# Six token blocks taken as three pairs, with seven half-width products for eight in their first channel product

## The chip, the core and the metric

The kernel runs on one core of a Trainium2 chip. Its time is the device time of that core in microseconds (us), the median of several runs. TensorE (PE) multiplies and adds up into PSUM banks; VectorE (DVE) and ScalarE (ACT) read PSUM and the core's on-chip memory SBUF, and GpSimd (POOL) here works on SBUF only; SyncE (SP) issues the transfers (DMAs), in order, from one queue. The engines run side by side and wait for each other on semaphores.

## The reference

`S` is 576, `B` is 8, `DM` is 512. Attention in chunks of 64 positions gives x; a token mixer and a channel mixer follow:

```python
scores = scale * np.matmul(q_c, k_c.transpose(0, 1, 2, 4, 3))
attn = np.exp(scores - np.max(scores, axis=-1, keepdims=True))
attn = attn / (np.sum(attn, axis=-1, keepdims=True) + 1e-09)
x = np.matmul(attn, v_c)                              # then [8, 576, 512]
h = np.maximum(x.transpose(0, 2, 1) @ w_tok1, 0.0) @ w_tok2   # 576 -> 256 -> 576
u = x + h.transpose(0, 2, 1)
out = u + np.maximum(u @ w_ch1, 0.0) @ w_ch2          # 512 -> 1536 -> 512
```

All data is 32-bit float. In the large products each operand is split into a high part and the rest (`xh`, `xl` and so on), and three of the four partial products are added up in PSUM (the tuple `THREE`), so each 128x128 by 128xN product costs three matmul instructions.

## The kernel before

**Stages.** Batch 0 goes first, in two halves of 288 positions, while the weights arrive and are converted and split. The positions of the other seven batches are one row of 4032, cut into `BLOCKS`: seven of 512 columns and one of 448. For each block, `turn` makes u by the second token product (`block_tok2`, line 562, ACT copy 573, rest on DVE or POOL 574). Then twelve steps `f`, one for each 128 of the 1536 hidden channels, run: `ch1` (line 584) multiplies four 128-channel tiles of u with the step's weights, 4 x 3 = 12 matmuls into one `ps_c1` bank; ACT takes the relu out of the bank (`gh`, line 595) and DVE the rest (`gl`, line 596); `ch2` (line 626), again 12 matmuls, adds the step into four `ps_acc` banks, one for each 128 output channels. `ch2` of a step runs one step behind `ch1`. At the end DVE adds u's high part to each bank (line 634), POOL its rest (line 636), and SP writes the result (line 637); for the last block POOL has added both parts of u beforehand (line 620), so only line 634 is left.

**Attention.** A tile of 128 rows needs a burst (`attention`): TensorE's 32 small matmuls for the scores of tile k (line 325) and 32 for the values of tile k-1 (line 337), both in the one `ps_at` bank pair. DVE then does the maximum, the subtraction, the scaled x of the older tile, two transposes, a sum and two small operations (lines 298 to 315, 348, 416), ACT the exponential (305); the transposed tiles go to DRAM and come back (`far`, `pf`, `xt`). Five or four bursts stand in each of the first six blocks (`SLOTS`). The first token product `tok1` (line 491) of a batch runs when its tiles are there.

**What sets the order.** TensorE's and SP's instructions stand in the order in which the program writes them. From batch 0's end on, DVE, ACT and POOL are ordered by a planner that places each instruction by its own estimate of when it can start; they then run in that fixed order, each waiting at its head. `ps_c1` has two banks, `ps_acc` four.

## Time and profile before

| | us |
|---|---|
| median of 3 runs (793.21 to 795.62) | 794.05 |
| the profiled execution, its time | 792.71 |
| its span, first to last instruction | 790.6 |
| TensorE busy | 774.0 |
| VectorE / ScalarE / GpSimd busy | 349.3 / 237.9 / 108.2 |

A span is what the trace sees of an execution. In views by group, `out<-in xcount | busy, mean ns of one | idle before`; "PE" is matmuls, "PEld" the loading of their weights, which runs beside them. Matmuls overlap: a "mean" of one is longer than the distance from one start to the next.

### The profile page before, as it was taken

To read this page: it belongs to the slowest core of one execution; us is meant where nothing else is said; L and a number is where in the kernel's file an instruction comes from. 1 tells how busy PE (TensorE), PEld (TensorE's weight loads), DVE (VectorE), ACT (ScalarE), POOL (GpSimd) and SP (SyncE) were. 2 spreads that over 40 slices of the span, in tenths; PEclk is the share of its full clock that TensorE was granted. 3 is DMA by queue.
4 is the path that set the end of the run, shared out by engine and by line. 5 is a ranking of instruction groups with operands and counts; after the bars stand their busy time and mean duration, and the time that the engine had idled before them with its cause. 6 is when DMAs were issued, how large, how long until landed. Compare 5 with 4: busy or idle time off the path is not lost.

```text
span 790.6 us, 14145 instructions
## 1 busy us (share of the span) xinstructions
PE 774.0 (98%) x5857; PEld 652.1 (82%) x5857; DVE 349.3 (44%) x627; ACT 237.9 (30%) x418; POOL 108.2 (14%) x94
## 2 busy tenths in 40 slices
PE   6899999999999999999999999999999999999998
PEld 4489898888888888888888888888888888888997
DVE  5888846654435341544444434535353314114112
ACT  6899834322221221222322222222212211101110
POOL 0000002310013010401040103100030103003300
PEclk8999999999999999999999999999999999999999
DMA  9934434343413440344413430535134201000101
GB/s 351 407 131 173 131 125 124 93 152 128 153 47 114 141 162 19 108 149 137 135 59 120 150 108 27 174 124 161 44 114 134 80 1 54 0 1 15 40 0 47
DMA packets 66415, 87.60 MB, mean 111 GB/s; under 512 B 7792, under 2 KB 41328, under 8 KB 66352
## 3 DMA queue, kind: packets, MB, share of 16 engines
q1 hardware_dynamic: 66352, 86.71, 33.0%
q8 instruction: 46, 0.75, 0.4%
q14 instruction: 17, 0.14, 0.1%
HBM read 59.81 MB, written 25.95 MB: 108 GB/s over the span
## 4 chain that ended last, share of the span: by engine, by line
PE 86%; DMA 5%; ACT 4%; DVE 3%; SPq 1%; issue 1%; DVEq 0%; ACTq 0%
PE acc L626 34%; PE ps_c L584 33%; PE ps_t L562 6%; PE ps_t L491 5%; DMA raw_c<-in_wc 2%; PE ps_sv L325 2%; PE ps_sv L337 2%; PE ps_t L534 1%; DMA v<-in_vo 1%; DMA far<-blocks 1%; ACT low L165 1%; PE ps_t L528 1%; SPq L359 1%; ACT low L174 1%; ACT wtop L164 1%
## 5 line engine op out<-in xcount | busy, mean ns | idle before, releaser
L626 PE MATMUL acc<-gh,kept_c 128*128 128x512 f32 (+2 forms) x960 | 272.8, 372 | 1.7 <-ACT gh L595 1.0
L584 PE MATMUL ps_c<-uh,kept_c 128*128 128x512 f32 (+1 forms) x768 | 234.1, 386 | 0.0
L596 DVE SCALAR_TENSOR_TENSOR gl<-ps_c,gh 128x512 fp32r<-128x512 f32 (+2 forms) x108 | 71.0, 657 | 315.4 <-ACT gh L595 315.4
L626 PEld LDWEIGHTS acc<-gh,kept_c 128*128 128x128 f32 x960 | 170.5, 188 | 30.9 <-ACT gh L595 1.5
L626 PE MATMUL acc<-gl,kept_c 128*128 128x512 f32 (+2 forms) x480 | 170.7, 369 | 0.0
L584 PEld LDWEIGHTS ps_c<-uh,kept_c 128*128 128x128 f32 x768 | 144.1, 188 | 27.5
L584 PE MATMUL ps_c<-ul,kept_c 128*128 128x512 f32 (+1 forms) x384 | 148.3, 386 | 0.0
L595 ACT ACTIVATE gh<-ps_c 128x512 fp32r<-128x512 f32 (+2 forms) x108 | 61.6, 570 | 283.6 <-PE ps_c L584 283.6
L626 PEld LDWEIGHTS acc<-gl,kept_c 128*128 128x128 f32 x480 | 88.0, 188 | 14.3
L434 POOL TENSOR_TENSOR xl<-x,xh 128x512 fp32r<-128x512 f32 x28 | 36.8, 1314 | 358.4 <-ACT xh L433 303.8
L584 PEld LDWEIGHTS ps_c<-ul,kept_c 128*128 128x128 f32 x384 | 72.1, 188 | 14.3 <-DVE ul L574 0.4
L574 POOL TENSOR_TENSOR ul<-u,uh 128x512 fp32r<-128x512 f32 (+1 forms) x16 | 20.9, 1307 | 256.3 <-ACT uh L573 219.3
L562 PE MATMUL ps_t<-kept_t,rh 128*128 128x448 f32 (+7 forms) x224 | 48.6, 311 | 0.0
L376 ACT COPY pt<-pf 128x512 f32<-128x512 f32 x31 | 19.2, 620 | 91.1 <-DMA pf<-far 91.1
L584 PE MATMUL ps_c<-both,kept_c 128*128 128x288 f32 x288 | 44.8, 302 | 0.2
L305 ACT ACTIVATE pr<-pr 128x512 f32<-128x512 f32 x36 | 22.7, 630 | 61.0 <-DVE pr L301 61.0
L584 PEld LDWEIGHTS ps_c<-both,kept_c 128*128 128x128 f32 x288 | 39.7, 188 | 1.5 <-ACT g L592 0.4
L562 PEld LDWEIGHTS ps_t<-kept_t,rh 128*128 128x128 f32 x224 | 37.6, 190 | 1.5
L636 POOL TENSOR_TENSOR o<-o,ul 128x512 f32<-128x512 f32 x28 | 38.5, 1404 | 1.2 <-DVE o L634 1.1
L568 DVE TENSOR_TENSOR u<-ps_t,xt 128x512 f32<-128x512 f32 (+1 forms) x32 | 21.8, 682 | 34.9 <-PE ps_t L562 34.7
L573 ACT CAST uh<-u 128x512 fp32r<-128x512 f32 (+1 forms) x32 | 19.5, 614 | 52.8 <-DVE u L568 52.8
L562 PE MATMUL ps_t<-kept_t,rl 128*128 128x448 f32 (+7 forms) x112 | 34.8, 311 | 0.0
(87 smaller groups left out, 701.3 us busy)
## 6 DMA issues: line engine op xcount, KB each, us to landing
qk<-in_qk SPq DMA_DIRECT2D x36, 512.0 KB, 3.9
far<-blocks SPq DMA_DIRECT2D x63, 256.0 KB, 2.1
raw_c<-in_wc SPq DMA_DIRECT2D x24, 512.0 KB, 9.3
pf<-far SPq DMA_DIRECT2D x124, 64.0 KB, 2.0
out<-o SPq DMA_DIRECT2D x28, 256.0 KB, 2.0
v<-in_v SPq DMA_DIRECT2D x27, 256.0 KB, 4.1
xt<-far SPq DMA_DIRECT2D x100, 64.0 KB, 2.0
v<-in_vo SPq DMA_DIRECT2D x9, 260.0 KB, 8.0
```

The lines of the kernel that those rows point to most:

```text
L305: nc.scalar.activation(out=pr, in_=pr, func=AF.Exp, scale=1.0 / float(D) ** 0.5)
L434: nc.gpsimd.tensor_tensor(out=xl, in0=t["x"], in1=xh.bitcast(F32), op=ALU.subtract)
L491: nc.tensor.matmul(ps, lhsT=lhsT, rhs=rhs, start=(n == 0 and q == 0), stop=(n == len(mt) - 1 and q == len(terms) - 1),)
L562: nc.tensor.matmul(ps[:, at:at + n], lhsT=lhsT[:, cols], rhs=rhs, start=(q == 0), stop=(q == len(terms) - 1),)
L568: nc.vector.tensor_tensor(out=u.rearrange("p (i c) -> p i c", c=BK), in0=ps[:, :width].rearrange("p (i c) -> p i c", c=BK), in1=block_x(k) ...
L573: nc.scalar.copy(out=uh[m], in_=u)
L574: (nc.vector if m in UL_ON_VECTOR else nc.gpsimd).tensor_tensor(out=ul[m], in0=u, in1=uh[m].bitcast(F32), op=ALU.subtract)
L584: nc.tensor.matmul(ps[:, :width], lhsT=weights["c1", f][:, wi, k * P:(k + 1) * P], rhs=u[ui][k], start=(k == 0 and q == 0), stop=(k == NDT ...
L595: nc.scalar.activation(out=gh, in_=ps[:, :width], func=AF.Relu)
L596: nc.vector.scalar_tensor_tensor(out=gl, in0=ps[:, :width], scalar=0.0, in1=gh.bitcast(F32), op0=ALU.max, op1=ALU.subtract)
L626: nc.tensor.matmul(accs[e], lhsT=weights["c2", f][:, wi, e * P:(e + 1) * P], rhs=g[gi], start=(f == 0 and q == 0), stop=(f == NFC - 1 and ...
L636: nc.gpsimd.tensor_tensor(out=o, in0=o, in1=u[1][e].bitcast(F32), op=ALU.add)
```

## The change

The first two blocks keep the old scheme. The six others are taken two at a time, in columns 512, 512 and 480 wide. For a pair of blocks and a pair of steps (2p, 2p+1), the first channel product is a 2x2 by 2x2 block product: two token blocks by two halves of 256 channels, times two halves by two steps. It is done by seven half-size products (`product`, 6 matmuls each into one `ps_c1` bank), with four combinations of u's quarters (`mix_pair`) and four of the weights' quarters (`add_sums`, `split_sums`). POOL and ACT make the weights' combinations during the two first blocks; SP writes all seven operands of each of the six step pairs to DRAM (`dump`, 42 tiles of 256 KB), and reads one before each product into a ring of 8 (`load_product`, 126 reads). The seven products are put together outside PSUM: `snap` copies two of them to SBUF on ACT, `plus` adds five more from PSUM on DVE and two sums in SBUF on POOL. The pair's first block gets its hidden steps at once (`c11`, `c21`), with its `ch2` in halves of 6 matmuls between the products; the second block's twelve are kept in SBUF (`later`) and its `ch2` follows in `pair_end`. The token weights are written to DRAM and read again for the pairs. Bursts stand nearer together, at places `step(0)` to `step(7)` of each p (14 in the two first blocks, 9 and 4 in the first two pairs' products), values two tiles behind scores (`LAG`).

```diff
 N = 512
-BLOCKS = [(k * N, min(N, (B - 1) * S - k * N)) for k in range(-(-(B - 1) * S // N))]
-SLOTS = {0: (1, 3, 5, 7, 9), 1: (2, 4, 6, 8), 2: (1, 3, 5, 7, 9)}
+SINGLE = 2
+PAIRS = 3
+BLOCKS = [(k * N, N) for k in range(2 * PAIRS)]
+LAST = ((B - 1) * S - 2 * PAIRS * N) // 2
+BLOCKS += [(2 * PAIRS * N + k * LAST, LAST) for k in range(2)]
+KH = 2 * P
+RING = 8
+LAG = 2
+BURSTS = (2, 5, 9, 13, 17, 21, 24, 27, 30, 32, 35, 38, 40, 43)
+PAIR_BURSTS = {0: (2, 7, 12, 17, 22, 27, 32, 37, 42), 1: (4, 12, 20, 28), 2: ()}
+PAIR_GAPS = (1, 3)
+SUMS = ((2, 5, 7), (8, 11, 13), (14, 17, 19), (24, 27, 29), (30, 33, 35), (36, 39, 41))
...
+    def before(k):
+        if LAG <= k:
+            with in_turn():
+                attn_t(order[k - LAG])
     def attention(k):
         i = order[k] if k < len(order) else None
-        j = order[k - 1] if k else None
-        if j is not None:
-            attn_t(j)
+        j = order[k - LAG] if k >= LAG else None
         attn_both(i, j)
+        if k + 2 < len(order):
+            attn_load(order[k + 2])
+        load_waiting(3)
         if i is not None:
             attn_p(i)
-            attn_far(i)
+            tiles[i]["far"] = far_out(tiles[i]["pr"])
             attn_z(i)
         if j is not None:
             attn_o(j)
             attn_end(j)
...
+    def behind(k):
+        if k < len(order):
+            t = tiles[order[k]]
+            t["pf"] = pool.tile([P, 4, NHP, BK], F32, tag="pf", name="pf", bufs=2)
+            far_in(t.pop("far"), t["pf"])
+        if LAG <= k:
+            j = order[k - LAG]
+            with in_turn():
+                stack_end(j)
+                if j in SOON:
+                    attn_split(j)
+    calls = {"before": before, "burst": attention, "behind": behind}
+    def plan_bursts(bursts, first, lead, trail):
+        at = {}
+        for k, s in enumerate(bursts, first):
+            for kind, t in (("before", s - lead), ("burst", s), ("behind", s + trail)):
+                at.setdefault(t, []).append((kind, k))
+        return at
...
+    def add_sums(p):
+        fa, fb = weights["c1", 2 * p], weights["c1", 2 * p + 1]
...
+        s = pool.tile([P, 4, KH], F32, tag="sums", name="sums", bufs=1)
+        for out_, in0, in1, op in (
+            (1, b[:, 0], b[:, 1], ALU.add), (0, s[:, 1], a[:, 0], ALU.subtract),
+            (2, a[:, 0], b[:, 0], ALU.subtract), (3, a[:, 1], s[:, 0], ALU.subtract),
+        ):
+            nc.gpsimd.tensor_tensor(out=s[:, out_], in0=in0, in1=in1, op=op)
...
+    def split_sums(p):
+        fa, fb, s = sources[p]
+        parts = pool.tile([P, 4, 2, KH], F32R, tag="sparts", name="sparts", bufs=1)
+        nc.scalar.copy(out=parts[:, :, 0], in_=s)
+        nc.gpsimd.tensor_tensor(
+            out=parts[:, :, 1], in0=s, in1=parts[:, :, 0].bitcast(F32), op=ALU.subtract
+        )
...
+    def dump(n):
+        for key, src in dumps[:n]:
+            stored[key] = wide.tile([P, 2, KH], F32, tag="w{}_{}".format(*key), name="w")
+            nc.sync.dma_start(out=stored[key], in_=src.bitcast(F32))
...
+    def load_product(upto):
+        for i in range(len(ring), min(upto, len(products))):
+            w = pool.tile([P, 2, KH], F32, tag="ring", name="ring", bufs=RING)
+            nc.sync.dma_start(out=w, in_=stored[products[i]])
+            ring.append(w)
...
+    def product(i, u, width):
+        load_product(i + RING - 1)
+        ps = ps_c1.tile([P, 512], F32, tag="c1", name="ps_p")[:, :width]
+        w = ring[i]
+        for j in range(2):
+            for q, (wi, ui) in enumerate(THREE):
+                nc.tensor.matmul(
+                    ps, lhsT=w[:, wi, j * P:(j + 1) * P].bitcast(F32R), rhs=u[ui][j],
+                    start=j == 0 and q == 0, stop=j == 1 and q == 2,
+                )
+        return ps
...
+    def mix_pair(k, rs, m):
...
+        for h, l in ((0, 0), (1, 0), (0, 1), (1, 1)):
...
+            us[h, l] = block_mix(k + l, rs, 2 * h + m, ps)
...
+        def combine(a, b):
+            t = pool.tile([P, N], F32, tag="ts", name="ts", bufs=4)[:, :width]
+            nc.vector.tensor_tensor(out=t, in0=a, in1=b, op=ALU.subtract)
+            return t
...
+            nc.scalar.copy(out=hi, in_=u)
+            engine.tensor_tensor(out=lo, in0=u, in1=hi.bitcast(F32), op=ALU.subtract)
...
+        split(0, us[0, 0], nc.vector)
+        split(1, us[1, 0], nc.gpsimd)
+        t1 = combine(us[0, 1], us[0, 0])
+        split(3, t1, nc.gpsimd)
+        t2 = combine(us[1, 1], t1)
+        split(2, t2, nc.gpsimd)
+        split(4, combine(us[1, 1], us[0, 1]), nc.gpsimd)
+        split(5, combine(us[1, 0], t2), nc.gpsimd)
+        split(6, us[1, 1], nc.gpsimd)
+        own["base"][m] = us[0, 1]
...
+    def finish(e, acc, at, width, base, rest=None):
+        o = pool.tile([P, N], F32, tag="o", name="o", bufs=8)[:, :width]
+        nc.vector.tensor_tensor(out=o, in0=acc, in1=base, op=ALU.add)
+        if rest is not None:
+            nc.gpsimd.tensor_tensor(out=o, in0=o, in1=rest, op=ALU.add)
+        nc.sync.dma_start(out=out[e, :, at:at + width], in_=o)
...
+    def snap(ps, width):
+        s = pool.tile([P, N], F32, tag="snap", name="snap", bufs=2)[:, :width]
+        nc.scalar.copy(out=s, in_=ps)
+        return s
...
+    def plus(a, b, width, tag, engine=None):
+        c = pool.tile([P, N], F32, tag=tag, name=tag, bufs={"g2": NFC, "sum": 3}.get(tag, 1))[:, :width]
+        (engine or nc.vector).tensor_tensor(out=c, in0=a, in1=b, op=ALU.add)
+        return c
...
+    def split_sum(c, width, relu=True):
+        gh, gl = g_parts(width)
+        nc.scalar.activation(out=gh, in_=c, func=AF.Relu)
+        nc.vector.scalar_tensor_tensor(
+            out=gl, in0=c, scalar=0.0, in1=gh.bitcast(F32), op0=ALU.max, op1=ALU.subtract
+        )
+        return gh, gl
...
+    def pair(n, rs):
...
+        for p in range(NFC // 2):
+            i = (n * (NFC // 2) + p) * 7
...
+            low, high = range(2), range(2, NDT)
+            p1 = snap(product(i, own[0], width), width)
+            c11 = plus(product(i + 1, own[1], width), p1, width, "c11")
+            step(0)
+            if pend is not None:
+                ch2_half(2 * p - 1, pend, accs, low, False, False)
+            step(1)
+            u2 = plus(product(i + 2, own[2], width), p1, width, "sum")
+            g1 = split_sum(c11, width)
+            p5 = snap(product(i + 3, own[3], width), width)
+            step(2)
+            if pend is not None:
+                ch2_half(2 * p - 1, pend, accs, high, False, False)
+            step(3)
+            u3 = plus(product(i + 4, own[4], width), u2, width, "sum")
+            u4 = plus(p5, u2, width, "sum", nc.gpsimd)
+            later[2 * p + 1] = plus(p5, u3, width, "g2", nc.gpsimd)
+            c21 = plus(product(i + 5, own[5], width), u3, width, "c21")
+            step(4)
+            ch2_half(2 * p, g1, accs, low, p == 0, False)
+            step(5)
+            pend = split_sum(c21, width)
+            later[2 * p] = plus(product(i + 6, own[6], width), u4, width, "g2")
+            step(6)
+            ch2_half(2 * p, g1, accs, high, p == 0, False)
+            step(7)
+            if p == NFC // 2 - 1 and n + 1 < PAIRS:
+                load_tokens(("t1", "half"))
+        ch2_half(NFC - 1, pend, accs, range(NDT), False, True)
+        for e in range(NDT):
+            h, m = divmod(e, 2)
+            finish(e, accs[e], S + at, width, own[h][0][m].bitcast(F32), own[h][1][m].bitcast(F32))
...
+    def pair_end(n, rs, later):
...
+        for f in range(NFC):
...
+            g, ahead = ahead, split_sum(later[f + 1], width) if f + 1 < NFC else None
+            ch2_half(f, g, accs, range(NDT), f == 0, f == NFC - 1)
+            for b, at_f in zip(mixes, (3, 5)):
+                if f == at_f:
+                    rs[b] = [tok1(b, m) for m in range(NT1)]
...
+            load_waiting(2)
+            if n + 1 < PAIRS and f in (6, 8):
+                load_waiting(99)
+                mix_pair(k + 2, rs, (f - 6) // 2)
+        for e in range(NDT):
+            h, m = divmod(e, 2)
+            if h == 0:
+                finish(e, accs[e], S + at, width, own["base"][m])
+            else:
+                finish(e, accs[e], S + at, width, own[6][0][m].bitcast(F32), own[6][1][m].bitcast(F32))
...
+    for k in range(SINGLE):
+        at, width = BLOCKS[k]
         accs, pend = [], None
         for f in range(NFC):
-            g = ch1(u, f, width=width)
-            if f in steps:
-                attention(done)
...
-            if pend is not None:
-                ch2(*pend)
-            pend = (S + at, width, u, f, g, accs)
-            if end and k + 1 < len(BLOCKS):
...
+            for half in range(2):
+                if half == 0:
+                    g = ch1(u, f, width=width)
+                elif pend is not None:
+                    ch2(*pend)
+                if half == 1:
+                    pend = (S + at, width, u, f, g, accs)
...
+                now = 2 * (NFC * k + f) + half
+                for kind, at_k in single_events.get(now, ()):
+                    calls[kind](at_k)
+                dump(2 if now > 36 else 1)
+                for p, (add, cut, put) in enumerate(SUMS):
+                    if now in (add, cut):
+                        with in_turn():
+                            (add_sums if now == add else split_sums)(p)
+                    if now == put:
+                        dump_sums(p)
+        dump(len(dumps))
+        if k == 0:
+            u = turn(1, rs)
+        else:
+            mix_pair(SINGLE, rs, 1)
+        ch2(*pend)
+    for n in range(PAIRS):
+        later = pair(n, rs)
+        pair_end(n, rs, later)
```

The three places on which the numbers rest, as the instructions are ordered. Names ending in a number are single buffers. **First, TensorE around a burst**, before, in step 2 of a block: the end of `ch1` (`ps_c1`), the burst (`ps_sv`), the start of `ch2` (`acc`).

```order
L584 MATMUL ps_c1_6394<-uh_6237,kept_c1_2_647 128x512 x2
L584 MATMUL ps_c1_6394<-ul_6241,kept_c1_2_647 128x512
L584 MATMUL ps_c1_6394<-uh_6238,kept_c1_2_647 128x512 x2
L584 MATMUL ps_c1_6394<-ul_6242,kept_c1_2_647 128x512
L325 MATMUL ps_sv_6413<-qk_6083 64x64 x16
L337 MATMUL ps_sv_6413<-v_5956,pt_6411 64x64 x16
L626 MATMUL acc_6378<-gh_6374,kept_c2_1_686 128x512 x2
L626 MATMUL acc_6378<-gl_6375,kept_c2_1_686 128x512
L626 MATMUL acc_6379<-gh_6374,kept_c2_1_686 128x512 x2
L626 MATMUL acc_6379<-gl_6375,kept_c2_1_686 128x512
```

And after, in the first pair, p = 1, at the burst behind the sixth product: the end of that product (`ps_p_4912`), the burst, half a `ch2`, and the seventh product (`ps_p_4989`).

```order
L996 MATMUL ps_p_4912<-bh_4568,ring_4753 128x512 x2
L996 MATMUL ps_p_4912<-bl_4569,ring_4753 128x512
L342 MATMUL ps_sv_4921<-qk_4689 64x64 x16
L354 MATMUL ps_sv_4921<-v_4104,pt_4893 64x64 x16
L1071 MATMUL acc_4604<-gh_4867,kept_c2_2_820 128x512 x2
L1071 MATMUL acc_4604<-gl_4868,kept_c2_2_820 128x512
L1071 MATMUL acc_4605<-gh_4867,kept_c2_2_820 128x512 x2
L1071 MATMUL acc_4605<-gl_4868,kept_c2_2_820 128x512
L996 MATMUL ps_p_4989<-bh_4464,ring_4828 128x512 x2
L996 MATMUL ps_p_4989<-bl_4465,ring_4828 128x512
L996 MATMUL ps_p_4989<-bh_4572,ring_4828 128x512 x2
L996 MATMUL ps_p_4989<-bl_4573,ring_4828 128x512
```

Twelve matmuls into one bank have become six, and a burst stands between short pieces.

**Second, DVE around a burst**, before: the twelve-matmul bank's rest (`gl`) stands ahead of and behind the burst's eight operations.

```order
L596 SCALAR_TENSOR_TENSOR gl<-ps_c_4773,gh 128x512
L298 TENSOR_REDUCE mx<-ps_sv 128x8
L301 TENSOR_TENSOR pr<-ps_sv,mx 128x2x4x64
L416 TENSOR_TENSOR x<-ps_sv,zs 128x512
L348 STREAM_TRANSPOSE blocks<-pr 128x4x4x32
L311 TENSOR_REDUCE zs<-pr 128x8
L348 STREAM_TRANSPOSE blocks<-x 128x4x4x32
L314 TENSOR_SCALAR zs<-zs 128x8
L315 RECIPROCAL zs<-zs 128x8
L596 SCALAR_TENSOR_TENSOR gl<-ps_c_4873,gh 128x512
```

And after, around the burst shown above. `sum` is the fifth product's addition, `c_4919` the sixth's, `g_4996` the seventh's.

```order
L1094 TENSOR_TENSOR sum<-ps_p,sum 128x512
L1094 TENSOR_TENSOR c_4919<-ps_p,sum 128x512
L1100 SCALAR_TENSOR_TENSOR gl<-c_4919,gh 128x512
L315 TENSOR_REDUCE mx<-ps_sv 128x8
L318 TENSOR_TENSOR pr<-ps_sv,mx 128x2x4x64
L433 TENSOR_TENSOR x<-ps_sv,zs 128x512
L365 STREAM_TRANSPOSE blocks<-pr 128x4x4x32
L328 TENSOR_REDUCE zs<-pr 128x8
L365 STREAM_TRANSPOSE blocks<-x 128x4x4x32
L1094 TENSOR_TENSOR g_4996<-ps_p,sum 128x512
L331 TENSOR_SCALAR zs<-zs 128x8
L332 RECIPROCAL zs<-zs 128x8
```

Three additions that read product banks have come in, one of them behind the burst's larger operations, and `gl` now reads SBUF (`c_4919`) where it read a bank.

**Third, the end**, before, on DVE (the last `gl`s, then the four output additions) and on POOL:

```order
L596 SCALAR_TENSOR_TENSOR gl<-ps_c_7712,gh 128x448
L596 SCALAR_TENSOR_TENSOR gl<-ps_c_7741,gh 128x448
L596 SCALAR_TENSOR_TENSOR gl<-ps_c_7770,gh 128x448
L596 SCALAR_TENSOR_TENSOR gl<-ps_c_7799,gh 128x448
L634 TENSOR_TENSOR o<-acc,o 128x448 x4
```

```order
L636 TENSOR_TENSOR o<-o,ul 128x512 x4
L574 TENSOR_TENSOR ul<-u,uh 128x448 x2
L636 TENSOR_TENSOR o<-o,ul 128x512 x2
L620 TENSOR_TENSOR o<-uh,ul 128x448 x4
L636 TENSOR_TENSOR o<-o,ul 128x512 x2
```

And after, DVE and POOL (its last six are four of the pair's first block and two of the second):

```order
L1100 SCALAR_TENSOR_TENSOR gl<-g_8312,gh 128x480
L1100 SCALAR_TENSOR_TENSOR gl<-g_8445,gh 128x480
L1100 SCALAR_TENSOR_TENSOR gl<-g_8417,gh 128x480
L1082 TENSOR_TENSOR o<-acc,u 128x480 x2
L1082 TENSOR_TENSOR o<-acc,bh 128x480 x2
```

```order
L1094 TENSOR_TENSOR sum<-snap,sum 128x480
L1094 TENSOR_TENSOR g_8312<-snap,sum 128x480
L1094 TENSOR_TENSOR sum<-snap,sum 128x480
L1094 TENSOR_TENSOR g_8417<-snap,sum 128x480
L1084 TENSOR_TENSOR o<-o,bl 128x480 x6
```

Two of the last four outputs now end with an addition on POOL, which before was done ahead of them.

More of the change, by code (lines that the diff above doesn't have):

```diff
@@ L468, in batch_tiles, with open_x, load_waiting, close_tile @@
+    def open_x(*blocks):
+        for k in blocks:
+            opened.add(k)
+            waiting.extend((i, k) for i in ended)
+    waiting = []
+    def load_waiting(n):
+        while waiting and n > 0:
+            n -= load_x(*waiting.pop(0))
+    ended = []
+    def close_tile(i):
+        ended.append(i)
+        waiting.extend((i, k) for k in sorted(opened))
     def batch_tiles(b):
@@ new lines, in load_tokens @@
+    def load_tokens(kinds):
+        for key, d in tokens.items():
+            if (key if key == "half" else key[0]) not in kinds:
+                continue
+            w = pool.tile(list(d.shape), F32, tag="again_" + "_".join(map(str, key)), name="again", bufs=1)
+            nc.sync.dma_start(out=w, in_=d)
+            w = w[:, :, :].bitcast(F32R)
+            if key == "half":
+                half_low[:] = [w[:, c] for c in range(2)]
+            elif key[0] == "t1":
+                for j in range(key[2]):
+                    weights["t1", key[1] + j] = w[:, :, j * DT:(j + 1) * DT]
+            else:
+                weights[key] = w
@@ new lines, in ch2_half, with new_accs @@
+    def ch2_half(f, g, accs, es, start, stop):
+        for e in es:
+            for q, (wi, gi) in enumerate(THREE):
+                nc.tensor.matmul(
+                    accs[e], lhsT=weights["c2", f][:, wi, e * P:(e + 1) * P], rhs=g[gi],
+                    start=start and q == 0, stop=stop and q == 2,
+                )
+    def new_accs(width):
+        return [ps_acc.tile([P, 512], F32, tag="acc", name="acc")[:, :width] for _ in range(NDT)]
+    def finish(e, acc, at, width, base, rest=None):
[4 more added lines that the diff above has]
+        nc.sync.dma_start(out=out[e, :, at:at + width], in_=o)
```

250 lines of the change are left out of this document (184 added, 66 removed).

## The prediction

> **What bounds the kernel now.** I read the busy table first, then busy time by stretch (columns: stretch, length, busy PE, PEld, DVE, ACT and POOL with counts, granted clock, DMA share, GB/s).
>
> ```profile
> span 790.6 us, 14145 instructions
> PE 774.0 (98%) x5857; PEld 652.1 (82%) x5857; DVE 349.3 (44%) x627; ACT 237.9 (30%) x418; POOL 108.2 (14%) x94
> ```
>
> ```profile
> 0.00:20.00 20.00, 14.01 (x225) 9.39 (x225) 10.29 (x25) 12.27 (x20) 0.91 (x10) 0.83 0.92 351
> 20.00:40.00 20.00, 16.42 (x194) 9.72 (x183) 15.96 (x36) 16.16 (x30) 0.00 (x0) 1.00 1.03 407
> 0.00:139.00 139.00, 126.51 (x1300) 107.50 (x1300) 100.10 (x209) 97.98 (x185) 9.85 (x18) 0.98 0.58 207
> 139.00:787.00 648.00, 647.50 (x4562) 544.63 (x4558) 248.51 (x418) 139.96 (x233) 98.31 (x77) 1.00 0.28 90
> 231.00:318.00 87.00, 87.00 (x640) 72.91 (x640) 34.41 (x58) 19.07 (x32) 14.52 (x11) 1.00 0.31 99
> ```
>
> All of TensorE's idle time but 0.5 us lies in the first 139 us and the last 4. Between, TensorE is the path, so a matmul less is time less, as long as nothing new makes it wait. Other engines have room there: in the block from 231 to 318 DVE is busy 34 of 87 us, POOL 15. The pace of TensorE stands in the chain of waits (start, length, what):
>
> ```profile
> 575.00 5.44 PE ps_c L584 x24
> ...
> 585.88 0.62 PE ps_sv L325 x32
> 586.51 0.47 PE ps_sv L337 x32
> ...
> 728.60 4.86 PE ps_c L584 x24
> ...
> 787.08 0.62 DVE o L634
> ```
>
> A matmul of 512 columns takes 5.44/24 = 0.2267 us, one of 448 takes 4.86/24 = 0.2025; on the line between them 480 columns take 0.2146. A burst takes 1.09.
>
> **Term 1, the matmuls removed: -24.0 us.** Before, the two channel products are 7 x 12 x 24 = 2016 matmuls of 512 and 288 of 448: 457.0 + 58.3 = 515.3 us. After, the two single blocks have 576 of 512; each of two pairs has 6 x 7 x 6 = 252 in products and 288 in `ch2`, so 1656 of 512 in all; the third pair has 540 of 480: 375.4 + 115.9 = 491.3. The other work of TensorE is kept: 27 bursts, 14 `tok1`, the second token product in equally many pieces. The first 139 us lose nothing on TensorE, so their idle time stays.
>
> **Term 2, the end: +2.1 us.** Before, the last DVE addition (787.08) is followed by its transfer. Now the third and fourth of the last outputs each get one more addition on POOL: 1.40 us for 512 columns (the POOL row on line 636 below), so 1.32 for 480. The third's can start when its DVE addition ends, 0.6 before the last one's, and the two follow each other: 2 x 1.32 - 0.6 = 2.1 later than now.
>
> **Term 3, waits for a product's bank: +2.4 us.** Groups (line, operation, count | busy, mean ns), then single instructions of DVE and ACT (start, length):
>
> ```profile
> L595 ACT ACTIVATE gh<-ps_c 128x512 fp32r<-128x512 f32 x84 | 50.2, 598 | 232.3 <-PE ps_c L584 232.3
> ...
> L634 DVE TENSOR_TENSOR o<-acc,uh 128x512 f32<-128x512 f32 x28 | 18.5, 684 | 0.4
> ...
> L434 POOL TENSOR_TENSOR xl<-x,xh 128x512 fp32r<-128x512 f32 x28 | 36.8, 1314 | 358.4 <-ACT xh L433 303.8 <-issue 32.8 <-PE acc L626 21.9
> ...
> L636 POOL TENSOR_TENSOR o<-o,ul 128x512 f32<-128x512 f32 x28 | 38.5, 1404 | 1.2 <-DVE o L634 1.1
> ```
>
> ```profile
> 241.66 0.39 PE L584 MATMUL ps_c<-ul,kept_c 128*128 128x512 f32 x1
> ...
> 242.15 0.60 ACT L595 ACTIVATE gh<-ps_c 128x512 fp32r<-128x512 f32 x1 [4.13 <-PE ps_c L584]
> ...
> 546.07 0.68 DVE L298 TENSOR_REDUCE mx<-ps_sv 128x8 f32<-128x512 f32 x1
> ...
> 550.23 0.20 DVE L315 RECIPROCAL zs<-zs 128x8 f32<-128x8 f32 x1
> ...
> 572.99 1.38 DVE L634 TENSOR_TENSOR o<-acc,uh 128x512 f32<-128x512 f32 x2
> 574.29 1.50 DVE L574 TENSOR_TENSOR ul<-u,uh 128x512 fp32r<-128x512 f32 x1
> 575.71 1.28 DVE L634 TENSOR_TENSOR o<-acc,uh 128x512 f32<-128x512 f32 x2
> ```
>
> A bank is handed over 0.10 us after its last matmul (242.05 to 242.15). It was emptied by `gh` and `gl` while 24 other matmuls, 5.4 us, ran; now a product's bank is wanted again after one product and half a `ch2`, 12 x 0.2267 = 2.72 us. Without a burst that fits: hand-over 0.10, then `snap` 0.60 (a copy out of PSUM, taken as `gh`) or a DVE addition with one PSUM operand, 0.69, then 0.10 back. At a pair's start, where there is no `ch2` yet, 1.36 against 0.9 still fits, and DVE has added the outputs of the block before by the first product's end.
>
> With a burst it is nearer. DVE is held 550.43 - 546.07 = 4.4 us. Take the burst of the rows in the change. With T the end of its matmuls, the sixth product ended at T - 1.09; `c` ends at T - 0.3, `gh` at T + 0.3, `gl` at T + 1.05; `mx`, `pr`, `x`, two transposes and `zs` take 4.0 more (the 4.4 without its two small last operations), so `g` ends at T + 5.75 and its bank is free at T + 5.85. TensorE asks for it after four pieces of 1.36, at T + 5.44: it waits 0.4 us. A burst after a step pair's second product gives the same for `sum`. There are six bursts at these two places (two in the first pair, the four of the second); at the other seven the next addition stands right behind `x`, or its bank has been emptied ahead of the burst. 6 x 0.4 = 2.4. Low end 0. High end: the addition behind `gl` and a whole burst at all 13 places, 3.1 us each as worked out in the rivals, 41 us. The written order is near the low end.
>
> `gl` now has both operands in SBUF. The 1.50 us row is such an operation beside POOL's work, and the additions from PSUM beside it stay at 0.69. If POOL were adding during the six `gl`s, they would cost 0.8 each, +4.9; but POOL's two sums of a step pair end about 0.6 us before that `gl` starts (the second follows the fifth product by 0.8 + 1.4), so I take 0.69. The Trainium skill (SBUF — State Buffer, "SBUF: two separate sides") says that a VectorE operation with two SBUF inputs and a GpSimd one exclude each other for a whole instruction. By it such a `gl` could take 0.69 + 1.40, and the six would give +8.4; the row shows 1.50, less than that.
>
> **Costed at nothing, with the cover.** *Weights' sums*: for each step pair POOL does two additions of 512, four of 256 and one of 1024 columns, about 3 x 2.6 = 8 us in proportion to the columns of the `xl` row, 48 for six, in two blocks, of which the second had POOL busy 14.5 of 87 us; without that room the first token products would wait for `xl`. *u's combinations*: in the second half of a mix POOL does six rests, and beside the first pair four output additions, 6 x 1.31 + 4 x 1.40 = 13.5 us, wanted for the seventh product about 16 us after they can start (the end of the mix, `ch2`, six products, half a `ch2` and a burst); each us beyond that is one us of waiting, at three pairs. *ACT* gains 36 snaps, 18 casts and six wide ones, about 40 us of 650. *DVE* gains 90 additions, 62 us: in the first pair, 99.6 us long, it has 5 additions and 2 `gl` in each of six step pairs and 9 bursts, 42 x 0.69 + 9 x 4.4 = 69 us (99.6 is 6 x 66 x 0.2267 + 9 x 1.09). *SP* gains 186 DMAs of 0.43 us:
>
> ```profile
> 239.41 4.54 SPq L637 DMA_DIRECT2D out<-o  x4
> ...
> 245.95 0.43 SPq L257 DMA_DIRECT2D qk<-in_qk  x1
> ```
>
> ```profile
> v<-in_v SPq DMA_DIRECT2D x27, 256.0 KB, 4.1
> ...
> raw_c<-in_wc SPq DMA_DIRECT2D x24, 512.0 KB, 9.3
> ```
>
> That is 80 us of issuing in some 630. The new transfers are 168 of 256 KB and 8 MB of token weights, 52 MB; with the 58 MB that 90 GB/s make in 648 us it is some 175 GB/s, and the start ran at 207. A ring read is issued seven products before its use, 12 to 15 us; a 256 KB read lands in 4.1. The attention tile's return (`pf`) moves behind loads and a second `far` on SP, but is used two bursts later, not one.
>
> **The sum.** 792.7 - 24.0 + 2.1 + 2.4 = 773.2 for the profiled execution; the median of the runs is 1.3 above it, so 794.05 - 19.5 = 774.5.
>
> **Rivals.** *The banks decide (slower).* The addition that reads a product stands behind `gl` and a burst on DVE: `gl` ends at T + 1.05, the burst's large operations 4.0 later, the addition 0.69, the way back 0.1, so the bank is free at T + 5.85. At most places it is wanted two pieces behind the burst, at T + 2.72: 3.1 us for each of 13 bursts, 41 us, and 794.05 - 24.0 + 2.1 + 41 = 813. It makes the change slower from 21.9/13 = 1.7 us a burst. For it: 4.4 us of burst against 2.72. Against: the additions are spread among the burst's operations.
> *The ring is late.* SP waits in order; outputs held it 4.54 us, and a read as slow as `raw_c` takes 9.3. Together 13.8, at a pair's start against 12.2, and some waits for DVE on top: 3 to 4 us at three pair starts, 785. Against: 4.1 is the size's own row.
> *The clock.* 20 to 40 us has 3.6 us of idle time at clock 1.00, 0 to 20 has 6.0 at 0.83. If the first pair's 99.6 us of short pieces ran at 0.83, that is 99.6 x (1/0.83 - 1) = 20.4 us: 795, no change. The Trainium skill (TensorE: Matmul & The Clock Gate, "A second HAM failure mode: psum-queue depth-cycling") tells of a matmul kernel whose clock swung because it idled briefly at each change of PSUM bank. Waits of 0.4 us are far from either row.
> *The matmuls saved are not time saved*: reading weights from the ring would have to cost 19.5/756 = 26 ns a matmul; 794. Against: PEld, busy 544.6 of 648 us, already runs beside the matmuls, and the ring's weights have the same shape.
>
> **How the numbers follow.** Forecast 0.74 (its own range 769.5 to 780), ring late 0.11, banks 0.09, clock 0.03, nothing saved 0.03. A change within 0.3%, about 2.4 us, is no change to this measurement. Faster: 0.74 + 0.11 = 0.85; same 0.06; slower 0.09. The low end of the range is term 1 alone, 770.0, less 0.5 for the scatter of the runs; the high end takes in the late ring, 785.
>
> **What would show it.** PE busy should fall to about 750, with 756 matmuls on the product line 0.2267 us apart. In the pairs, idle time of PE under about 5 us, ended by DVE's additions, and near the step-4 and step-0 bursts; more than 22 us makes me wrong. PE's waits for the ring's DMAs: none. Granted clock 1.00 there. The chain of waits should end with POOL's addition, about 2 us more behind the last matmul. If idle time lies in the two single blocks, the sums or the writing on SP are to blame.

## The result: half a per cent slower, not 2.5% faster

Measured over 16 executions each, the change takes 798.48 us (median, 791.52 to 803.76) and the kernel before 793.27 (791.57 to 796.23): 1.0054 times the time, 95% interval 1.0034 to 1.0074. The ratio is of means and leaves out the change's two longest executions (803.59 and 803.76 us), which count as slow, so it lies a little below that of the medians. Forecast were 774.5 us. The profiled execution of the change took 795.3 us, its span is 793.5.

The head of the page of the change:

```profile
span 793.5 us, 14680 instructions
PE 760.0 (96%) x5749; PEld 636.0 (80%) x5749; DVE 445.3 (56%) x735; ACT 269.9 (34%) x478; POOL 234.3 (30%) x190
PE 74%; DMA 7%; DVE 7%; SPq 4%; ACT 3%; POOL 3%; issue 2%; POOLq 0%; DVEq 0%; ACTq 0%
```

The 108 matmuls are gone (5857 to 5749), but TensorE's busy time fell by 14.0 us, not 24, and its idle time rose from 16.6 to 33.5. In the chain of waits (third line) TensorE's part, 86% before, is 74%; DMA, DVE and SP's queue have gained. Busy time by stretch (columns as before: stretch, length, busy PE, PEld, DVE, ACT, POOL, granted clock, DMA share, GB/s), first the kernel before:

```profile
152.00:231.00 79.00, 78.53 (x643) 63.93 (x642) 34.46 (x64) 19.88 (x33) 10.26 (x9) 1.00 0.41 127
231.00:340.00 109.00, 109.00 (x800) 91.35 (x800) 46.26 (x77) 24.36 (x40) 22.68 (x17) 1.00 0.32 103
```

and the change:

```profile
152.00:231.00 79.00, 76.00 (x674) 61.24 (x673) 38.59 (x68) 22.61 (x37) 32.55 (x30) 0.96 0.72 236
231.00:340.00 109.00, 103.47 (x946) 85.48 (x945) 56.56 (x95) 31.20 (x53) 41.42 (x35) 1.00 0.67 214
340.00:380.00 40.00, 33.18 (x276) 27.88 (x276) 28.02 (x37) 12.38 (x21) 27.21 (x18) 0.91 0.38 125
380.00:787.00 407.00, 406.04 (x2454) 341.37 (x2453) 208.64 (x305) 101.29 (x175) 119.17 (x86) 1.00 0.47 150
420.00:460.00 40.00, 40.00 (x410) 32.53 (x410) 27.05 (x48) 10.57 (x18) 6.44 (x5) 1.00 0.84 262
```

The start is as it was (TensorE busy 127.25 us of the first 139, before 126.51). In the pairs TensorE waits 1 us in all (406.04 of 407), although the first pair's DMA engines are busy 84% of the time. Nearly all that was lost lies between 152 and 380 us: in the two single blocks and at the step into the first pair. The blocks' transfers about doubled, from 127 and 103 to 236 and 214 GB/s. TensorE's longest waits there (start, length, what; in brackets the idle time ahead and what ended it):

```profile
178.64 0.73 PE L691 MATMUL acc<-gh,kept_c 128*128 128x512 f32 x2 [0.79 <-ACT gh L660]
181.21 0.79 PE L691 MATMUL acc<-gl,kept_c 128*128 128x512 f32 x1 [1.83 <-DVE gl L661]
...
349.60 0.69 PE L621 MATMUL ps_t<-kept_t,rh 128*128 128x128 f32 x2 [4.20 <-DVE u L627]
356.59 0.47 PE L621 MATMUL ps_t<-kept_t,rh 128*128 128x192 f32 x2 [0.93 <-DVE u L627]
367.29 0.50 PE L996 MATMUL ps_p<-bl,ring 128*128 128x512 f32 x1 [0.74 <-POOL bl L1052]
373.96 0.50 PE L996 MATMUL ps_p<-bl,ring 128*128 128x512 f32 x1 [0.95 <-POOL bl L1052]
```

Left out are waits of 1.48, 1.61 and 1.91 us at 299, 307 and 319 us, two for `pt`, the tile that comes back from DRAM, and two short ones. The engines named are not the cause. ACT's rows, and DVE's, show what those stood for:

```profile
173.11 1.26 ACT L480 CAST xr<-xc 64x512 fp32r<-64x512 f32 x2 [6.11 <-DMA xc<-x]
...
297.40 1.05 ACT L955 CAST sparts<-sums 128x1024 fp32r<-128x1024 f32 x1 [2.93 <-DMA w<-sparts]
...
317.48 1.05 ACT L955 CAST sparts<-sums 128x1024 fp32r<-128x1024 f32 x1 [7.89 <-DMA w<-sparts]
...
347.60 0.62 ACT L1051 CAST bh<-u 128x512 fp32r<-128x512 f32 x1 [10.87 <-DMA w<-kept_c]
348.25 0.69 DVE L1052 TENSOR_TENSOR bl<-u,bh 128x512 fp32r<-128x512 f32 x1 [9.70 <-ACT bh L1051]
```

ACT works in its fixed order. At 173 us its next instruction was a cast of the stacked tile, and waited for that tile's transfer `xc`; the exponential, `gh`, and with them DVE's `gl`, stood behind. DVE's subtraction of the same tile waited with it (6.68 us), ahead of the burst's own operations. At 347 us it was the mix's first `bh`, which lies where the weights lay, and so waited for the last write of weights to DRAM; DVE's `bl` waited for `bh`, and the other `u` additions behind `bl`, with TensorE, for that. The wait for `pt` at 299 us is of the same kind: its `pf` had been issued by 294.45 (in this stretch they land within 2.7 us), and ACT stood until 297.40 before the write that frees `sparts`, the one buffer of split sums, with `pt` behind. Ahead of the wait at 319 us ACT stood 7.89 us before such a write, but there `pf` was itself issued only by 317.30. SP's rows tell why the transfers at 173 and 347 us were late:

```profile
158.53 4.24 SPq L1009 DMA_DIRECT2D wt<-kept_t  x5
162.82 1.18 SPq L1009 DMA_DIRECT2D wt<-half_low  x1
...
168.81 2.33 SPq L471 DMA_DIRECT2D xc<-x  x2
...
338.97 3.43 SPq L986 DMA_DIRECT2D ring<-w  x7
342.74 0.32 SPq L977 DMA_DIRECT2D w<-kept_c  x1
```

The six token-weight writes stand ahead of `xc`, and seven ring reads ahead of the last write: the rate of two writes per half step leaves one over.

**The account.** By the matmuls' own pace 22.9 us were saved (24.0 less 540 x 0.0021, since 480 columns take 0.2167, below), so TensorE would be busy 751.1; it was 760.0. That is 8.9 us slower running, in step with the granted clock of the whole execution, 0.986 for 0.996, which is 7.9 us of 793. Idle time is up by 33.5 - 16.6 = 16.9 us: 14.4 in the nine waits quoted or named, 1.8 at the end, the rest in short ones. 16.9 + 8.9 - 22.9 = 2.9, the difference of the spans.

### The profile page after: what moved, and what is told of

Same layout as the page of the kernel before. It is cut to its first block, busy times and chain, and to the rows that moved or that the text cites. A ratio compares the mean times of both kernels' runs of the same rounds, so it can differ in the third digit from the quotient of the medians.

```text
span 793.5 us, 14680 instructions
## 1 busy us (share of the span) xinstructions
PE 760.0 (96%) x5749; PEld 636.0 (80%) x5749; DVE 445.3 (56%) x735; ACT 269.9 (34%) x478; POOL 234.3 (30%) x190
## 4 chain that ended last, share of the span: by engine, by line
PE 74%; DMA 7%; DVE 7%; SPq 4%; ACT 3%; POOL 3%; issue 2%; POOLq 0%; DVEq 0%; ACTq 0%
PE acc L1071 23%; PE ps_p L996 21%; PE acc L691 8%; PE ps_c L649 7%; PE ps_t L551 6%; PE ps_t L621 4%; DMA raw_c<-in_wc 2%; DVE ts L1045 2%; PE ps_sv L342 2%; DMA far<-blocks 2%; SPq L376 1%; PE ps_sv L354 1%; PE ps_t L594 1%; POOL bl L1052 1%; POOL o L701 1%
## 5 line engine op out<-in xcount | busy, mean ns | idle before, releaser
L1071 PE MATMUL acc<-gh,kept_c 128*128 128x512 f32 (+1 forms) x576 | 176.4, 387 | 0.0
L996 PE MATMUL ps_p<-bh,ring 128*128 128x512 f32 (+1 forms) x504 | 154.1, 387 | 0.0
L1071 PE MATMUL acc<-gl,kept_c 128*128 128x512 f32 (+1 forms) x288 | 111.1, 386 | 0.0
L996 PEld LDWEIGHTS ps_p<-bh,ring 128*128 128x128 f32 x504 | 94.1, 188 | 18.5 <-DVE g L1094 0.5
L691 PE MATMUL acc<-gh,kept_c 128*128 128x288 f32 (+1 forms) x384 | 96.6, 350 | 3.2 <-ACT gh L660 2.0
L996 PE MATMUL ps_p<-bl,ring 128*128 128x512 f32 (+1 forms) x252 | 97.4, 386 | 1.7 <-POOL bl L1052 1.7
L691 PE MATMUL acc<-gl,kept_c 128*128 128x288 f32 (+1 forms) x192 | 61.0, 348 | 1.8 <-DVE gl L661 1.8
L649 PE MATMUL ps_c<-uh,kept_c 128*128 128x512 f32 x192 | 60.4, 396 | 0.5 <-DVE rl L569 0.5
L996 PEld LDWEIGHTS ps_p<-bl,ring 128*128 128x128 f32 x252 | 47.3, 188 | 11.6 <-POOL bl L1052 2.5
L649 PEld LDWEIGHTS ps_c<-uh,kept_c 128*128 128x128 f32 x192 | 35.2, 188 | 8.4 <-DVE rl L569 1.0
```

The costliest lines, as they stand in the source:

```text
L649: nc.tensor.matmul(ps[:, :width], lhsT=weights["c1", f][:, wi, k // 2, k % 2 * P:(k % 2 + 1) * P], rhs=u[ui][k], start=(k == 0 and q == 0) ...
L691: nc.tensor.matmul(accs[e], lhsT=weights["c2", f][:, wi, e * P:(e + 1) * P], rhs=g[gi], start=(f == 0 and q == 0), stop=(f == NFC - 1 and ...
L996: nc.tensor.matmul(ps, lhsT=w[:, wi, j * P:(j + 1) * P].bitcast(F32R), rhs=u[ui][j], start=j == 0 and q == 0, stop=j == 1 and q == 2,)
L1071: nc.tensor.matmul(accs[e], lhsT=weights["c2", f][:, wi, e * P:(e + 1) * P], rhs=g[gi], start=start and q == 0, stop=stop and q == 2,)
```

## The experiments

Ratios are to the kernel before, run alongside, with 95% intervals; times are medians; 1.0054 and 798.5 us are the change's. The theory after the traces: the writes of weights, which I had costed at nothing on SP, make TensorE wait in the single blocks. The rivals: POOL's sums, and the banks.

**1. Few writes; no sums.** First, 33 of the 42 writes left out; second, the 48 operations on sums:

```diff
-            stored[key] = wide.tile([P, 2, KH], F32, tag="w{}_{}".format(*key), name="w")
-            nc.sync.dma_start(out=stored[key], in_=src.bitcast(F32))
+            w = wide.tile([P, 2, KH], F32, tag="w{}_{}".format(*key), name="w")
+            full = key[0] == 0 and key[1] in (0, 1, 5)
+            if full or key[1] == 6:
+                nc.sync.dma_start(out=w, in_=src.bitcast(F32))
+            if full:
+                stored.update({(p, n): w for p in range(NFC // 2) for n in range(7) if n % 3 == key[1] % 3})
```
```diff
-            (2, parts[:, 0]), (3, parts[:, 1]), (4, parts[:, 2]), (6, parts[:, 3]),
+            (2, fa[:, :, 0]), (3, fa[:, :, 1]), (4, fb[:, :, 0]), (6, fb[:, :, 1]),
...
-                            (add_sums if now == add else split_sums)(p)
+                            pass
```

> Of the 42 writes of weights and their sums to DRAM only 9 are left (three whose tiles all later reads use, and one of each step pair's sums, which keeps the sums alive); sums, reads, token-weight writes and all arithmetic stay in kind and number, so the output is not the reference's. Theory (the writes on SP's queue make TensorE wait): the waits near 295-320 us and the 4.2 us wait before the first mix of a pair go, with the half-clock stretch behind the latter: 7.4 + 4.4 + 2.4 = 14 us less than the change, about 784; the gap near 178 us, which the token-weight writes make, stays. Rival (POOL's sums): no gain, 798. Rival (banks or contention inside the pairs): 798.

> The weights' sums and their splitting (42 operations of POOL, 6 of ACT) are left out and weight tiles are written in their place, so as many writes and reads as in the change, and an output that is not the reference's. Theory (writes): at most 2 us less than the change, 796 to 798, with the waits near 178, 299, 318 and 345 us still there. Rival (the sums): the 14 us lost between 152 and 340 us come back, 784.

783.6 us, 0.9896 (0.9847 to 0.9945), and 797.2 us, 1.0059 (1.0037 to 1.0081). The theory's numbers, 784 and 796 to 798, came out; the sums cost next to nothing. Busy time by stretch, with few writes:

```profile
231.00:340.00 109.00, 108.99 (x992) 91.58 (x991) 63.33 (x103) 34.87 (x60) 48.16 (x40) 1.00 0.54 172
380.00:460.00 80.00, 77.36 (x677) 62.59 (x676) 50.94 (x88) 22.86 (x39) 15.88 (x12) 0.96 0.78 260
```

The second single block has no idle time left, with POOL busier than before (48.16 us). A wait of 2.6 us for `pt` at 405 us, in the first pair, is new; ACT had stood 4.90 us before another `xc` there, with `pt` behind.

**2. Small writes.** All 42 stay in the queue, 39 of them with 8 of the 128 partitions:

```diff
...
+            rows = P if full else 8
+            nc.sync.dma_start(out=w[:rows], in_=src[:rows].bitcast(F32))
```

> All 42 writes stay on SP's queue, but 39 of them carry 8 of the 128 partitions, 16 KB for 256; the reads all take three tiles that are written whole, so the output is not the reference's. Theory A (the bytes: the writes delay the attention tiles' transfers on the DMA engines): as with few writes, 784. Theory B (the issuing: SP takes 0.43 us for each and works in order): no gain over the change, 797 to 799. Both in part: in between.

786.7 us, 0.9929 (0.9910 to 0.9949): of the 15 us, 12 go with the bytes. The other 3, which would be the issuing, are inside the two intervals. In the trace the last write, small as it is, still stands behind the seven ring reads: ACT waited 8.32 us before it and TensorE 1.64 us at 340.

**3. The last write first; the token weights spread**, one of their six tiles at each call of `store_tokens`.

```diff
-                dump(2 if now > 36 else 1)
+                dump(3 if now > 41 else 2 if now > 36 else 1)
```
```diff
-    store_tokens()
...
                 dump(2 if now > 36 else 1)
+                store_tokens()
```

> Three writes per half step instead of two from half step 42 on, so that the last write of weights is issued ahead of the seven first ring reads instead of behind them. Theory: the 4.2 us wait of TensorE before the first pair's mix (345.4 to 349.6) was ACT's bh waiting for that write, whose source lies where bh is put; it shrinks below 1 us and the half clock behind it goes, 4.2 + 2.4 = 6 to 7 us less, about 792. Rival (u waits for the late loads of x): no change, 798.

> The six writes of token weights, issued together at 158 us, are issued one per half step in the first six half steps of the first single block. Theory: the idle time of 2.6 us near 178 us and the half clock that follows it go, 6 us less, about 792. Rival (ACT and DVE are simply behind there, by the sums or the stacked tile): the gap stays, 798.

The last write first: 791.0 us, 0.9962 (0.9935 to 0.9988), 7.5 less, as expected. The wait of 4.2 us is gone, and so is the low clock at that place (1.00 for 0.91 in this stretch):

```profile
340.00:380.00 40.00, 38.30 (x310) 32.27 (x309) 32.01 (x46) 14.64 (x25) 27.44 (x19) 1.00 0.54 175
```

Token weights spread: 795.6 us, 1.0030 (1.0006 to 1.0053), 3 less and not 6, and its interval overlaps the change's. The gap near 178 us went, but a wait of 3 us came in the first pair:

```profile
152.00:231.00 79.00, 77.53 (x694) 63.18 (x693) 39.52 (x68) 23.67 (x40) 33.31 (x31) 1.00 0.77 252
```

The cause of that wait, in the rows of ACT and TensorE:

```profile
417.75 1.26 ACT L480 CAST xr<-xc 64x512 fp32r<-64x512 f32 x2 [5.32 <-DMA xc<-x]
...
420.06 0.69 PE L354 MATMUL ps_sv<-v,pt 64*64 64x64 f32 x32 [3.03 <-ACT pt L393]
```

The next stacked tile's `xr` waited for its `xc`, now with `pt` behind it.

**4. Writes earlier.** The 18 writes that need no sum go to steps 0 to 8 of the second half of batch 0, with the token weights behind them (first edit), or to steps 6 to 11 of the loop before, with the token weights spread (second edit); both with the last write first:

```diff
+        for key in early[2 * f:2 * f + 2]:
+            store_weight(*key)
```
```diff
+        for e in (2 * f - 12, 2 * f - 11) if f >= 6 else ():
+            for j in (1,) if e % 2 else (0, 1):
+                store_weight(e, j)
```

> The 18 writes of weights that need no sum are issued two per step in steps 0 to 8 of the second half of the first product (about 100 to 138 us, where the DMA share is 0.3 to 0.6), the token weights two per step in steps 9 to 11; the last writes three per half step. All results as in the reference. Theory (writes in the single blocks are to blame): the waits near 178, 299, 318 us shrink and the one of 4.2 us goes: 798.5 - 6 - 7 - 7 = 778 to 783. Rival (the writing costs the same wherever it stands): waits of TensorE appear before 150 us, 791 as with the last write first alone.

> The 18 writes of weights that need no sum stand in steps 6 to 11 of the first loop (about 80 to 125 us), three a step, ahead of the waits of SP's queue that held them back when they stood a loop later; the token weights go one per half step in the first single block, the last sums three per half step. Results as in the reference. Theory (in the single blocks SP's queue and the transfers are too full): the waits of TensorE near 178 us go, those at 299 to 318 us shrink, that of 4.2 us is gone: 798.5 - 6 - 5 - 7 = 780. Rival (the queue delays the attention tiles wherever writes stand in it): waits of TensorE at 80 to 130 us, more than 5 us of them, 790.

800.8 us, 1.0104 (1.0070 to 1.0137), and 796.6 us, 1.0042 (1.0020 to 1.0064): the gain of the last write was lost again. SP's rows of the first:

```profile
152.78 1.75 SPq L376 DMA_DIRECT2D pf<-far  x4
154.58 4.66 SPq L929 DMA_DIRECT2D w<-kept_c  x8
159.28 3.82 SPq L922 DMA_DIRECT2D wt<-kept_t  x4
...
165.14 0.49 SPq L370 DMA_DIRECT2D far<-blocks  x1
170.28 1.75 SPq L376 DMA_DIRECT2D pf<-far  x4
```

A queue that waits in order does not issue where the program means it to: `pf` was held for its `far`, issued at 147.88 us, and eight writes came out behind it at 154 us, with four token weights; the next tile's `far` stood behind all twelve, and TensorE waited 4.67 us at 170 for its `pt`. In the loop before, the writes met a queue with more room, but TensorE waited 1.1 and 2.2 us there for what stood behind them, and 4.75 at 174 for a `pt`, with ACT 8.74 us ahead of an `xr` in front of it.

On the first, one kernel moved the stacked tile's casts a half step, where they still stood ahead of `pt` in ACT's order, and one opened the loads of x two steps sooner as well. On the second, one moved the casts behind `pt`, and one opened x as well:

> As the kernel with early writes, and the casts and subtractions of the stacked tile (ACT xr, DVE stack) come one half step later in the single blocks and two pieces later in the pairs. Theory: ACT, which works in order, waits up to 6 us for the transfer xc ahead of gh and of the next tile's pt; later, the transfer has landed: 2 to 5 us less than with early writes alone, and no wait of TensorE near 178 or 417 us. Rival (the waits there come from elsewhere): the same time as with early writes alone.

> As the kernel before it, and the loads of x for the first pair are opened at step 1 of the second single block instead of step 3, so they are spread over two more bursts. Theory (SP's queue is full from 265 to 343 us, bursts of 12 loads take 6.8 us): the waits near 299 and 318 us go, 2 to 4 us less than the kernel before it. Rival: the loads are needed no sooner and only delay others, same time.

> As the kernel before it, with the stacked tile's casts and subtractions one half step (a piece, in the pairs) later and behind the next tile's pt in ACT's order, not ahead of it. Theory (ACT waits in order for xc): no wait of TensorE for pt near 168, 297 and 417 us, 2 to 4 us less than the kernel before it. Rival (pt itself is late, its transfer pf): same time as the kernel before it.

> As the kernel before it, and the loads of x for the first pair opened at step 1 of the second single block for step 3. Theory (SP's queue is full in the second half of that block): the waits near 299 to 318 us go, 1 to 4 us less. Rival: same time.

1.0123 (1.0094 to 1.0152) and 1.0160 (1.0143 to 1.0176): no better, the second worse; in the first ACT stood 17.0 us ahead of `xr`. Behind `pt`: 789.6 us, 0.9963 (0.9950 to 0.9976), 7 less than without; x sooner on top: 793.2 us, 1.0011 (0.9996 to 1.0025). By these times ACT's order pays, and x sooner costs. The trace does not show how the 7 us came about: near 178 us the cast, now ahead of `pr` and `gh`, stood 6.59 us before its `xc`, and TensorE waited 1.26 and 1.83 us there, about as in the change. The next experiment puts the cast behind `pr`.

**5. Only the order on ACT, only the rate.** From the change, with the last write first: the casts behind the next burst's `pr`; or two writes each half step, meant to finish the write that frees `sparts` before ACT's next cast into it:

```diff
-    for kind, t in (("before", s - lead), ("burst", s), ("behind", s + trail)):
+    for kind, t in (("before", s - lead), ("burst", s), ("behind", s + trail), ("stacked", s + trail + more)):
...
+    single_events = plan_bursts(BURSTS, len(FIRST_QK), 1, 1, 2)
```
```diff
-                dump(2 if now > 36 else 1)
+                dump(3 if now > 41 else 2)
```

> The last write first, and the stacked tile's casts and subtractions behind the next burst's pr on ACT; token weights in one piece at 158 us as in the change. Theory (ACT waits for xc ahead of gh and pr): the wait and the half clock near 178 us go though the token writes stay, 791 - 6 = 785. Rival (the token writes themselves delay what TensorE waits for): the gap stays, 791.

> Only the rate of the writes is changed, two per half step, three from half step 42 on. Theory: the last write's 7 us, and 3 to 4 us of the waits at 299 to 318 us, where ACT's cast into sparts waited for the write of the sums before: 787. Rival (that wait of ACT costs nothing): 791, as with the last write first alone.

Stack alone: 786.2 us, 0.9919 (0.9893 to 0.9944), 5 less than with the last write first, as expected (the intervals just overlap), with the token weights still in one piece (two stretches):

```profile
152.00:231.00 79.00, 78.62 (x702) 64.36 (x701) 38.36 (x68) 23.89 (x40) 33.41 (x31) 1.00 0.78 261
231.00:340.00 109.00, 102.97 (x937) 85.17 (x936) 62.09 (x98) 31.26 (x52) 42.24 (x35) 0.95 0.67 215
```

The gap at 178 us and its low clock are gone though no byte was moved: there it was ACT's place in its order, with DVE's, whose subtractions moved along. A row of ACT from the second stretch shows the same thing once more, 9 us before a write, and right behind it TensorE's waits of 4.02 us for `pt` and 2.01 for `gl`:

```profile
291.29 1.04 ACT L963 CAST sparts<-sums 128x1024 fp32r<-128x1024 f32 x1 [9.06 <-DMA w<-sparts]
```

The rate alone gave 790.2 us, 0.9972 (0.9953 to 0.9991), the rival's 791 rather than 787.

**6. All three, and more.** Rate, spread token weights and the moved casts together; then the outputs of the second block behind the mix; two buffers of `sparts`; x one tile per half step; the last two together:

> From the change: two writes per half step in the single blocks (three from half step 42 on), so that a pair's sums are written before the next ones are split; token weights one per half step from the first on; the stacked tile's casts and subtractions one half step later, behind the next burst's pr on ACT; no writes in the first loop. Results as in the reference. Theory (TensorE waits because ACT, in order, stands before a transfer - xc or the write that frees sparts or the place of bh - and gh, pr and pt stand behind it): the waits near 178, 299 to 318 and 345 us shrink to 3 us in all: 798.5 - 6 - 5 - 7 = 780 to 782. Rival (the transfers pf themselves are late, whatever ACT does): 787 to 790, as with the best kernel so far.

> As the kernel with all three, and the last output additions of the second single block stand behind the first mix's operations on POOL, DVE and ACT. Theory: the two waits of TensorE for POOL's bl at the first pair's start (0.7 and 1.0 us) go, 1 to 2 us less than the kernel with all three. Rival: the banks of acc come free later instead, same time.

> As the kernel with all three, and the split sums (sparts) have two buffers instead of one, so that ACT's cast does not wait for the write of the pair before. Theory (ACT stood 9 us before that write, with gh and pt behind it, where the stacked tile alone was moved): the waits of TensorE left in the second single block, 280 to 310 us, shrink from 4 us to 1 or 2: 782. Rival (these waits are for pf's transfer): same time as with all three, 785.

> As the kernel with all three (one buffer of sparts), and the loads of x for the next blocks go one tile per half step and one per burst instead of three per burst. Theory (SP issues 12 of them in 7 us and the sums' writes and far stand behind): those waits shrink by 2 to 3 us, 782. Rival (the queue was not what they waited for): same, 785.

> Two buffers of sparts and x spread, with all three. Theory: TensorE waits under 2 us between 152 and 340 us and 1.7 us at the first pair's start; 780. Rival (each takes away the same waits): as the better of the two alone.

All three: **785.1 us, 0.9900 (0.9883 to 0.9917)**, faster than the kernel before and than the change, though the interval overlaps that of the moved casts alone. Outputs behind: 786.9 us, 0.9932 (0.9908 to 0.9957). Two buffers: 785.4 us, 0.9920 (0.9896 to 0.9944). X spread: 800.7 us, 1.0103 (1.0090 to 1.0116), and with two buffers 802.7 us, 1.0133 (1.0100 to 1.0165). The page's head of the kernel with all three, then a stretch:

```profile
span 781.7 us, 14670 instructions
PE 754.4 (97%) x5749; PEld 631.6 (81%) x5749; DVE 451.3 (58%) x735; ACT 269.5 (34%) x478; POOL 234.8 (30%) x190
```
```profile
231.00:340.00 109.00, 104.83 (x959) 86.56 (x957) 60.21 (x100) 32.20 (x53) 43.64 (x37) 1.00 0.66 210
```

TensorE runs 754.4 us, 3.3 above its own pace; 4 us of waits are left in the second block. Most of them, 1.66 us before 282.4 and 1.26 before 309.2, end with a `gl`; its `gh` stood behind ACT's cast into `sparts`, which still waited for a write (and 2.13 us at 306):

```profile
280.07 1.05 ACT L963 CAST sparts<-sums 128x1024 fp32r<-128x1024 f32 x1 [7.43 <-DMA w<-sparts]
```

With two buffers ACT no longer stands there, but the time is the same: in that trace (of the longest of its five executions) ACT waits 5.74 us for a `pf` at 304 us instead, and TensorE 2.66 for the `pt`. Spreading x did not test its bursts alone, and made it much worse: SP then holds `pf` behind an `xt` load, which itself waits for the `far` issued at 299.71 us, and TensorE waits 4.35 us for that tile's `pt`:

```profile
299.71 0.86 SPq L370 DMA_DIRECT2D far<-blocks  x2
305.34 1.74 SPq L376 DMA_DIRECT2D xt<-far  x4
307.19 1.79 SPq L376 DMA_DIRECT2D pf<-far  x4
```

## Why the prediction was wrong, step by step

- **Term 1** was right in kind, 108 matmuls and, at 2.72 us for 12, an unchanged pace in the pairs. Of its size 1.1 us was lost: 480 columns take 0.2167 us (33.81 for the last 156), not the 0.2146 of the line between 448 and 512.

```profile
383.97 2.72 PE ps_p L996 x12
...
752.95 33.81 PE acc L1071 x156
```

- **Term 2** was right. From the last matmul's end, 787.67 + 0.38 in the first row, to the span's end are 5.45 us, before 790.6 - 786.97 = 3.63: 1.8 more, for 2.1. POOL's two additions took 1.17 each, not 1.32:

```profile
787.67 0.38 PE L1071 MATMUL acc<-gl,kept_c 128*128 128x480 f32 x1
788.17 2.34 POOL L1084 TENSOR_TENSOR o<-o,bl 128x480 f32<-128x480 f32 x2 [26.90 <-DVE o L1082]
```

- **Term 3** did not show: no wait for a product's bank in the pairs, 0 for 2.4 us. `gl` in the products of 512 columns took 0.75 us on average (24 of them) for the 0.69 taken, and TensorE did not wait for it there; in the pairs' second blocks, where it had no price of its own, it took 1.06. The rivals of the banks, of the clock in the first pair, and of saved matmuls not being saved time are refuted by the rows of the pairs (406.04 of 407 us, clock 1.00, 2.72 us for 12). The late ring did not happen in the change; where outputs stood behind the mix it cost 2.29, 0.80 and 0.21 us.
- **"Costed at nothing" failed, at SP.** The step was "that is 80 us of issuing in some 630", and 175 GB/s on average. Neither is a cover. All the writes, and 14 of the attention's bursts, lie in the 190 us of the single blocks; there the DMA engines were 0.72 and 0.67 busy, and in the second block a `far` took 3.6 us to land for 2.1 before, an `xt` load 4.8 for 2.0. Instructions of ACT stood before such transfers, for 6.11 us at 173 and 10.87 at 347 above all, with TensorE's next operand behind. Without 33 of the 42 writes the kernel takes 783.6 us, 15 less. Nor had the sum a term for the clock that fell behind the waits: 8.9 us of slower running, 7.9 by the granted clock. The prediction named what to look for, "if idle time lies in the two single blocks, the sums or the writing on SP are to blame"; it was the writing. The rows, in the stretch of 231 to 340 us, of the kernel before and then the change (tile, count, size, median us to landing):

```profile
far<-blocks SPq DMA_DIRECT2D x10, 256.0 KB, 2.1
xt<-far SPq DMA_DIRECT2D x18, 64.0 KB, 2.0
```
```profile
far<-blocks SPq DMA_DIRECT2D x16, 256.0 KB, 3.6
xt<-far SPq DMA_DIRECT2D x24, 64.0 KB, 4.8
```

- **u's combinations.** DVE's four subtractions of a mix (`ts`, two SBUF operands) had no price at all. Beside POOL they took up to 1.80 us, where 0.7 was the least. What came of it is small: 0.93 us for `u`, 0.74 and 0.95 for `bl` at the first pair, 0.84 for `u` at the second, no wait at the third.
- **The 48 us of sums on POOL** were rightly costed at nothing: without them the kernel took 797.2 us for 798.5.

The writes do not explain all of the miss: the kernel with few writes (783.6) is still 8 us above the forecast with Term 1 put right (775.6). Its trace has waits of 1.84 us at 179, 1.78 at the first pair's start and 2.60 at 405, the last followed by a low clock; how the 8 us divide among these and the clock was not tested. What also stays open is what would take away the last 4 us of waits in the second single block: in the one trace in which ACT no longer stands before `sparts`, `pf` is late. A run in which the writes leave SP's queue for another one was not made.

## What to carry to other kernels

Price a queue and an in-order engine in the stage where the work lands, not over the whole run: bytes, issues, and who stands behind the instruction that will wait for them. Busy time does not show this; ACT was 34% busy and held TensorE at 178 and 345 us, for 6.8 us. When a transfer gets slower, a cheap mend is to put the instruction that waits for it behind those that TensorE needs next. That gave 5 us without moving a byte. Issuing the one write that ACT waited for ahead of the ring reads gave 7.5; moving 18 other writes earlier only moved the waits.
